# Raw weight blocks placed in another pool and requested at another point, and eight plain matmuls at a group's end

## The chip, the cores and the metric

One core of a Trainium2 chip runs the whole program. The metric is the device time of one execution in microseconds; the number used for a kernel is the median over its runs. A profile of one execution shows what every engine does: TensorE (PE, with its weight loads as PEld), VectorE (DVE), ScalarE (ACT), GpSimd (POOL), SyncE (SP) and the DMA queues that SP and POOL issue to.

## What is computed

Three layers follow each other. First a linear recurrence per head over 768 steps with complex decays (4 batches, 8 heads, head size 48), then a layer that sends each of 3072 tokens to one of 8 experts, then a product of two projections followed by two more weight matrices:

```python
# layer 1: S is 48x48 per batch and head
for t in range(768):
    new_re = ar * S_re - ai * S_im          # ar, ai: a_re, a_im, cut to magnitude 0.999
    new_im = ar * S_im + ai * S_re
    S_re, S_im = new_re + outer(k[t], v[t]), new_im
    y[t] = q[t] @ S_re
# layer 2: for the tokens of expert e (argmax of x @ w_gate), gate = softmax value of that expert
out[mask] = gate * (relu(x[mask] @ w1[e]) @ w2[e])       # 384 -> 1024 -> 384
# layer 3
h = ((x @ w1) * (x @ w2)) @ w3                           # 384 -> 1024, then 1024 x 1024
return h @ w_out                                         # 1024 -> 384
```

The weights of layer 3 come as float64.

## The kernel before

**Layer 1** is done by two streams that `drive` interleaves in the program's order. The stream `first` (`Attn.elementwise`, L803) goes through 24 pieces of 8 time steps: it forms the decay coefficients `cf` (L840) from `a`, `sq` and `y0`, multiplies them up to prefix products `P` (L861, L863), scales queries and keys by them into `qk` (L903) and stores that to DRAM as `qkd` (POOL L910 and L912, for the last half piece SP L916 and L917 and POOL L918). The tiles `a`, `sq`, `y0` and `cf`, which the text calls the multipliers' memory, live in the pool `e`; `P`, `pr`, `s2` and the raw queries and keys live in the pools `e2` and `qk`.

The stream `second` (`Attn.groups`, L1126) goes through three groups of the sequence, each of 8 units of 64 steps for 2 batches. A unit loads `vz` and `kk` (L1007, L1009, on SP), transposes `kk` (L993) into `qkT` (ACT L994), forms scores in the PSUM tile `sc` (L1021) which DVE masks (L1025), and forms the outputs `y` (L1040, L1041; the last matmul is remembered as `self.lasty`). Units are tied by a state `W` in PSUM: PE adds the last state by L1078, ACT copies it out (`z`, L1079), PE adds the unit's keys and values (L1085), ACT and DVE multiply it by the decays (L1092, L1093, L1094), and L1078 of the next unit waits for that. A group can start when its 8 pieces are stored (`made`); at its start `ends` (L967) transposes the last prefixes and, ahead of the second and of each earlier group only (`g < NG - 1`), runs 8 plain matmuls named `dense`, whose result nobody reads. Finished rows are routed to their experts by `route` (L111) and scattered by POOL (L162).

**Layer 3's inner product**, `w3 @ w_out`, is formed ahead of layer 2 by the class `Fuse`. Its inputs are 24 raw float64 blocks: 8 of `w_out` (384 KB each) and 16 halves of `w3` (512 KB each). SP loads a raw block (`doubles`, L291) into one of five buffers `fdr`; `halves` (L313) makes two float32r parts of it with six DVE operations (L336, L337, L339, then L322, L323, L324) and two of ACT (L329, L330); this is called a split below. `ahead` (L278) keeps up to four loads ahead of the split that is being written. The first 16 splits (8 of `w_out`, 4 pairs of `w3`) are taken one or two at a time by the third group's loop (L1165 to L1167), the other 8 behind the last routing. `_bound` (L711) places every DVE operation of the first 16 splits behind `S.end`, the last `qk` multiplication (L903).

The pool `wf1` (`wp`) is opened by `factors`, when the 24th piece's prefixes are written into the program and the pool `e` is closed; in memory it takes the place of `e`. The pool `wf2` (`w2p`) is opened when `first` is through and takes the place of `e2` and `qk`. In the kernel before, `wf1` holds both parts of all eight `w_out` factors and one pair of `w3` parts, `wf2` holds the five raw buffers and three pairs of `w3` parts.

**The order of work** on each engine is fixed when the program is built: a scheduler takes each instruction as its inputs, its memory and its engine come free by its own model of time, earlier program lines first. Each engine then runs its list in order, waiting where an input is not there. So an SP load that waits for a buffer holds up the loads behind it, and a DVE split that waits for a raw block holds up the chain's DVE operations behind it.

After the last unit, PE runs the product of six `w3` blocks (L729), then the experts with the rest of the product in between (L478), and then layer 3 (L538).

Of the kernel before, what the change touches and what calls it, by code (L numbers as in the profile page):

```python
# [9 lines left out]
F32 = mybir.dt.float32  # L10
F32R = mybir.dt.float32r
# [10 lines left out]
DM = 384  # L22
# [3 lines left out]
NF = 8  # L26
# [6 lines left out]
RAW = 4  # L33
# [241 lines left out]
        yield  # L275


def ahead(load, srcs, n):  # L278

    got = []  # L280
    for i in range(len(srcs)):
        while len(got) < min(i + n, len(srcs)):
            got.append(load(srcs[len(got)]))
        yield got[i]


def doubles(pool, dma, bufs=RAW):

    def load(src):
        raw = pool.tile([128, 512, 2], I32, tag="fdr", name="fdr", bufs=bufs)[:, : src.shape[-1]]  # L290
        dma.dma_start(raw.rearrange("p n c -> p (n c)"), src.bitcast(I32))  # L291
        return raw

    return load
# [18 lines left out]
def halves(S, nc, raws, rest, units):  # L313

    v, act = nc.vector, nc.scalar
    first, second = [], []
    for n in range(len(units) + 2):
        if second:
            place, raw, m = second.pop()
            H, L = place()  # L320
            hi, lo = raw[:, :, 1].bitcast(F32), raw[:, :, 0].bitcast(F32)
            v.tensor_tensor(out=H, in0=hi, in1=m.bitcast(F32), op=ALU.mult)  # L322
            v.tensor_scalar(out=m, in0=H.bitcast(I32), scalar1=-0x800000, scalar2=None, op0=ALU.bitwise_and)  # L323
            v.scalar_tensor_tensor(out=L, in0=lo, scalar=2.0 ** -20, in1=m.bitcast(F32), op0=ALU.mult, op1=ALU.mult)  # L324
        if first:
            second.append(first.pop())
            _, raw, m = second[0]
            hi = raw[:, :, 1].bitcast(F32)
            act.activation(out=m, in_=m, func=AF.Relu, scale=8.0, bias=S.rebias)  # L329
            act.activation(out=hi, in_=hi, func=AF.Sign)  # L330
        if n < len(units):
            raw = next(raws)
            k = raw.shape[1]
            m = rest.tile([128, 512], I32, tag="fdm", name="fdm", bufs=2)[:, :k]
            low = rest.tile([128, 512], U16, tag="fdl", name="fdl")[:, :k]
            v.tensor_scalar(out=m, in0=raw[:, :, 1], scalar1=0x7FFFFE00, scalar2=None, op0=ALU.bitwise_and)  # L336
            v.tensor_scalar(out=low, in0=raw.bitcast(U16)[:, :, 2], scalar1=0x1FF, scalar2=None, op0=ALU.bitwise_and)  # L337
            lo = raw[:, :, 0]
            v.scalar_tensor_tensor(out=lo.bitcast(F32), in0=lo.bitcast(U32), scalar=2.0 ** -32, in1=low, op0=ALU.mult, op1=ALU.add)  # L339
            first.append((units[n], raw, m))  # L340
        yield
# [7 lines left out]
def mm3(nc, out, lh, ll, rh, rl, first, last):  # L349
    nc.tensor.matmul(out, lh, rh, start=first, stop=False)  # L350
    nc.tensor.matmul(out, lh, rl, start=False, stop=False)  # L351
    return nc.tensor.matmul(out, ll, rh, start=False, stop=last)  # L352


class Expert:


    def __init__(self, tc, S, wp, xp, hp, ps, py):
        self.nc, self.S = tc.nc, S
        self.wp, self.xp, self.hp, self.ps, self.py = wp, xp, hp, ps, py  # L360
# [79 lines left out]


def moe(tc, S, fuse, product):

    nc = tc.nc
    extra = moe2_weights(tc, S)
    with ExitStack() as pools:
# [55 lines left out]
        for x in (product, extra):  # L502
            for _ in x:
                pass
# [116 lines left out]
NH = 8  # L621
# [3 lines left out]
NG = 3  # L625
# [4 lines left out]
R2 = 2 * D  # L630
# [10 lines left out]
WARM = 8  # L641
# [30 lines left out]
class Fuse:  # L672


    def __init__(self, tc, S, wp, psum):

        self.tc, self.S, self.nc, self.wp = tc, S, tc.nc, wp
        self.psum = psum
        self.w2p = None
        self.ready = self.blocks = 0  # L680
        self.units = self._singles()

    def _singles(self):
        nc, S, wp = self.nc, self.S, self.wp
        self.wo = [wp.tile([128, NF, DM], F32R, tag=f"wo{x}", name=f"wo{x}") for x in "hl"]
        self.w3 = []

        def factor(f):
            return lambda: [x[:, f] for x in self.wo]

        def block(f, h):
            def place():
                if not h:
                    pool = wp if f % W3B == 0 else self.w2p
                    self.w3.append([pool.tile([128, NF, 128], F32R, tag=f"w3{x}{f % W3B}", name=f"w3{x}{f}") for x in "hl"])
                return [x.rearrange("p g c -> p (g c)")[:, h * 512 : (h + 1) * 512] for x in self.w3[f]]
            return place

        srcs = [S.w_out[f * 128 : (f + 1) * 128, :] for f in range(NF)]
        srcs += [S.w3[f, :, h * 512 : (h + 1) * 512] for f in range(NF) for h in range(2)]  # L700
        raws = ahead(doubles(self.w2p, nc.sync, 5), srcs, 4)
        first = [factor(f) for f in range(NF)] + [block(f, h) for f in range(W3B) for h in range(2)]
        rest = [block(f, h) for f in range(W3B, NF) for h in range(2)]
        for n, _ in enumerate(self._bound(halves(S, nc, raws, wp, first), lambda: [S.end])):
            self.ready = max((n - 1 - NF) // 2, 0)
            yield
        for n, _ in enumerate(self._bound(halves(S, nc, raws, wp, rest), lambda: S.gate)):
            self.ready = W3B + max((n - 1) // 2, 0)
            yield

    def _bound(self, steps, behind):  # L711
        while True:
            with ExitStack() as order:
                for x in behind():
                    order.enter_context(self.tc.issue_after(x.ins))
                if next(steps, self) is self:
                    return
            yield

    def product(self):  # L720
        nc = self.nc
        for f in range(NF):
            while self.ready <= f:
                next(self.units)
                yield 0
            wh, wl = self.w3[f]
            po = self.psum(f, f"wpo_{f}")
            for g in range(NF):
                mm3(nc, po[:, :DM], wh[:, g], wl[:, g], self.wo[0][:, g], self.wo[1][:, g], g == 0, g == NF - 1)  # L729
                if g % 2 and g < NF - 1:  # L730
                    if self.ready < min(f + W3B, BEFORE):
                        next(self.units)
                    yield 960
            ws = (self.wp if f % 2 else self.w2p).tile([128, DM], F32, tag="ws", name=f"ws_{f}")
            nc.scalar.copy(ws, po[:, :DM])
            nc.sync.dma_start(self.S.wf[f * 128 : (f + 1) * 128, :], ws)
            self.blocks = f + 1
            yield 960
# [38 lines left out]
class Attn:  # L777
# [251 lines left out]
    def outputs(self, u, v, z):  # L1029
        nc, S, st, pp = self.nc, self.S, self.st, self.pp  # L1030
        g, q, c = u
        nm = "%d%d%d" % u
        qkT, at = self.qkT.pop(u), self.at.pop(u)
        y = pp.tile([128, NH, D], F32, tag="y", name=f"y{nm}")
        for h in range(NH):
            for i in range(2):
                ps = slice(i * C, (i + 1) * C)
                nz = g == 0 and c == 0
                if not nz:
                    nc.tensor.matmul(y[ps, h], qkT[:, 0, h, ps], z[:, h // 4, i, h % 4], start=True, stop=False)  # L1040
                self.lasty = nc.tensor.matmul(y[ps, h], at[:, h], v[:, i, h], start=nz, stop=True)  # L1041
            if h == NH - 1:
                xt = S.rpool.tile([128, DM], F32, tag="xo", name=f"xo{nm}", bufs=S.xbufs)
                nc.scalar.copy(xt, y.rearrange("p h d -> p (h d)"))
                self.held.pop(u)
                self.xs.append((tuple((2 * q + i) * SEQ + (g * 4 + c) * C for i in range(2)), xt))
                if len(self.xs) == (RB if g == NG - 1 else RB0):
                    bank = lambda name: self.adds.tile([128, 512], F32, tag="ad", name=name, bufs=2)
                    at = max([n for n, x in enumerate(self.pool) if x.kind == "route"], default=0)
                    ids, xts = zip(*self.xs)  # L1050
                    number(self.tc, S, self.slot, ids)
                    self.pool.insert(at + 1, Item("route", self.route(self.slot, xts, bank)))
                    self.slot += len(self.xs)
                    self.xs = []
            if h % 2:
                yield 650
# [259 lines left out]
W3B = 4  # L1316
# [113 lines left out]
```

## Time and profile before

| what | us |
|---|---|
| median of 3 runs (lowest, highest) | 1000.34 (997.92, 1002.75) |
| the profiled execution, its own time | 1002.27 |
| its span, first to last instruction | 1000.6 |
| PE busy in the span | 900.3 |
| DVE busy in the span | 608.9 |
| ACT busy in the span | 488.9 |
| mean granted TensorE clock | 0.943 |

The span is read in stages: layer 1 up to 404.6 us, the inner product and the routing's end up to 434 us, the experts up to some 700 us, layer 3 to the end. A stage in which PE is busy nearly all the time can only become shorter by less PE work or a higher clock; in layer 1, PE is not, and the engine or the transfer that ends PE's idle time must be looked up for each stretch. The granted clock is given as a share of the higher of two levels: 1.00 is 2.4 GHz, 0.50 is 1.2 GHz, and a number in between says how much of the stretch lay at either.

### The profile page before, as it was taken

What the parts mean: (1) busy time and instruction counts of PE and PEld (TensorE: products, weight loads), DVE (VectorE), ACT (ScalarE), POOL (GpSimd) and SP (SyncE); (2) the same over time, 40 slices, a digit from 0 to 9 for tenths busy, and PEclk for the clock granted to TensorE, in tenths of its full rate; (3) what the DMA queues carried; (4) which work ended last, traced back from release to release, by engine and by line L of the source; (5) the groups of instructions that cost most, each with busy time, mean ns of one, the idle gap of its engine ahead of it and who ended that gap; (6) DMA issues with size and microseconds to landing.
All of it is one profiled execution on the core that took longest, in us unless ns stands there. A gap on an engine that the chain in (4) does not pass through costs nothing. (4 is left out here: it accounts for less than half of the span.)

```text
span 1000.6 us, 17074 instructions
## 1 busy us (share of the span) xinstructions
PE 900.3 (90%) x6402; PEld 769.4 (77%) x6402; DVE 608.9 (61%) x1378; ACT 488.9 (49%) x1092; POOL 129.1 (13%) x198
## 2 busy tenths in 40 slices
PE   3446799967998979999989999998999999999997
PEld 2222478746886868989979999997888888888886
DVE  6999899997993885666589995442232323232222
ACT  6555689865774766445456654443131313121211
POOL 5111000211020100100242211110000000000001
PEclk8766999978997999999999999999999999999999
DMA  6566975348728763644687745630000000000000
GB/s 221 179 206 236 293 247 172 122 128 290 226 112 279 215 216 102 204 141 122 183 222 173 205 113 136 138 68 2 1 9 24 9 24 9 24 7 27 9 24 31
DMA packets 90246, 128.74 MB, mean 129 GB/s; under 512 B 7264, under 2 KB 72720, under 8 KB 90160
## 3 DMA queue, kind: packets, MB, share of 16 engines
q1 hardware_dynamic: 76316, 82.42, 28.9%
q0 software_dynamic: 10736, 40.56, 11.6%
q10 hardware_dynamic: 3108, 4.65, 1.7%
q8 instruction: 51, 0.84, 0.3%
q14 instruction: 35, 0.29, 0.1%
HBM read 92.38 MB, written 35.22 MB: 128 GB/s over the span
## 5 line engine op out<-in xcount | busy, mean ns | idle before, releaser
L606 DVE TENSOR_TENSOR ab<-asb,pb 128x512 f32<-128x512 f32 x48 | 33.0, 687 | 189.8 <-PE pb L352 184.7
L345 ACT CAST h<-w 128x384 fp32r<-128x384 f32 x128 | 65.4, 514 | 96.8 <-PE ph L351 50.6
L346 DVE TENSOR_TENSOR l<-w,h 128x384 fp32r<-128x384 f32 x128 | 70.6, 555 | 63.3 <-ACT h L345 60.5
L601 ACT COPY asb<-pa 128x512 f32<-128x512 f32 x48 | 28.2, 587 | 122.6 <-PE pa L352 117.0
L345 ACT CAST gh<-ab 128x512 fp32r<-128x512 f32 x48 | 29.7, 620 | 95.2 <-DVE ab L606 95.2
L817 PE MATMUL x<-s,ident 128*128 128x384 f32 x64 | 36.0, 701 | 43.7 <-ACT s L876 43.7
L351 PE MATMUL py<-hl,h 128*128 128x432 f32 x192 | 70.7, 368 | 4.1 <-DVE hl L407 4.1
L993 PE MATMUL tr<-ident,kk 128*96 128x128 f32 x384 | 62.3, 298 | 10.5 <-DMA kk<-qkd 10.5
L350 PE MATMUL py<-hh,h 128*128 128x432 f32 x192 | 69.6, 363 | 2.2 <-ACT hh L406 2.2
L352 PE MATMUL py<-hh,l 128*128 128x432 f32 x192 | 69.6, 362 | 0.0
L350 PE MATMUL ph<-xh,h 128*128 128x432 f32 x192 | 69.1, 361 | 0.0
L352 PE MATMUL ph<-xh,l 128*128 128x432 f32 x192 | 69.1, 360 | 0.0
L351 PE MATMUL ph<-xl,h 128*128 128x432 f32 x192 | 68.9, 359 | 0.0
L861 DVE TENSOR_TENSOR pr<-cf,P 128x192 f32<-128x192 f32 x189 | 66.6, 353 | 3.3
L994 ACT COPY qkT<-tr 96x512 f32<-96x512 f32 x96 | 54.9, 593 | 23.3 <-PE tr L993 22.7
L351 PE MATMUL po<-ol,gh 128*128 128x384 f32 x192 | 65.0, 338 | 0.0
L350 PE MATMUL po<-oh,gh 128*128 128x384 f32 x192 | 64.8, 338 | 0.0
L352 PE MATMUL po<-oh,gl 128*128 128x384 f32 x192 | 64.0, 338 | 0.0
L570 POOL DMA_INDIRECT out<-ob,mdp x24 | 23.8, 992 | 307.4 <-DVE ob L569 165.6
L350 PE MATMUL pa<-yh,ah 128*128 128x512 f32 x144 | 57.3, 398 | 3.0 <-ACT yh L345 3.0
L993 PEld LDWEIGHTS tr<-ident,kk 128*96 128x96 f32 x384 | 44.4, 138 | 19.8 <-DMA kk<-qkd 8.4
L817 PEld LDWEIGHTS x<-s,ident 128*128 128x128 f32 x64 | 14.9, 258 | 58.1 <-ACT s L876 50.8
(219 smaller groups left out, 2410.8 us busy)
## 6 DMA issues: line engine op xcount, KB each, us to landing
w<-in_w SPq DMA_DIRECT2D x128, 192.0 KB, 2.6
kk<-qkd SPq DMA_DIRECT2D x24, 768.0 KB, 7.6
qkd<-qk POOLq DMA_DIRECT2D x21, 768.0 KB, 5.7
qkr<-in_qk SPq DMA_DIRECT2D x24, 384.0 KB, 6.5
a<-in_a SPq DMA_DIRECT2D x11, 768.0 KB, 5.6
fdr<-in_w SPq DMA_DIRECT2D x16, 512.0 KB, 5.6
fdr<-in_v POOLq DMA_DIRECT2D x12, 512.0 KB, 6.9
xs<-zr POOLq DMA_DIRECT2D x8, 648.0 KB, 7.2
```

The lines of the kernel that those rows point to most:

```text
L345: nc.scalar.copy(H, src)
L346: nc.vector.tensor_tensor(out=L, in0=src, in1=H.bitcast(F32), op=ALU.subtract)
L350: nc.tensor.matmul(out, lh, rh, start=first, stop=False)
L351: nc.tensor.matmul(out, lh, rl, start=False, stop=False)
L352: return nc.tensor.matmul(out, ll, rh, start=False, stop=last)
L570: nc.gpsimd.indirect_dma_start(out=S.outv[j], out_offset=bass.IndirectOffsetOnAxis(ap=S.mdp[:, j, 0:1], axis=0), in_=ob, in_offset=None, b ...
L601: nc.scalar.copy(asb, pa)
L606: nc.vector.tensor_tensor(out=ab, in0=asb, in1=pb, op=ALU.mult)
L817: nc.tensor.matmul(p, S.ident, s[r], start=r == 0, stop=r == 1)
L861: v.tensor_tensor(out=pr, in0=twice(cf[i][:, t]), in1=bc(pv, 2, 1), op=ALU.mult)
L993: nc.tensor.transpose(pt[:, h], qk[:, h0 + h, w], self.S.ident)
L994: nc.scalar.copy(qkT[:, w, h0 : h0 + 4], pt)
```

## The change

The five raw buffers move from `wf2` to `wf1`, and the first five loads are written into the program as soon as `wf1` is open, ahead of the last piece's keys and stores and of the third group's loads. To make room, the factors 4 to 7 of `w_out` and the pair of `w3` parts that lay in `wf1` move to `wf2`. The splits themselves, their order in the program and their place behind `S.end` stay as they are. Besides, behind the last output of the second group's last unit (`u == (1, 1, 3)`), eight matmuls of 512 columns are added that write to a tile in the bank of the scores; nobody reads it.

```diff
-def ahead(load, srcs, n):
-
-    got = []
+def ahead(load, srcs, n, got=()):
+
+    got = list(got)
...
         self.w2p = None
         self.ready = self.blocks = 0
+        self.srcs = [S.w_out[f * 128 : (f + 1) * 128, :] for f in range(NF)]
+        self.srcs += [S.w3[f, :, h * 512 : (h + 1) * 512] for f in range(NF) for h in range(2)]
+        self.load = doubles(wp, self.nc.sync, RAW + 1)
+        self.first = [self.load(x) for x in self.srcs[: RAW + 1]]
         self.units = self._singles()
...
-        self.wo = [wp.tile([128, NF, DM], F32R, tag=f"wo{x}", name=f"wo{x}") for x in "hl"]
+        n = NF // 2
+        self.wo = [[p.tile([128, n, DM], F32R, tag=f"wo{x}", name=f"wo{x}{i}") for x in "hl"] for i, p in enumerate((wp, self.w2p))]
...
-                    pool = wp if f % W3B == 0 else self.w2p
-                    self.w3.append([pool.tile([128, NF, 128], F32R, tag=f"w3{x}{f % W3B}", name=f"w3{x}{f}") for x in "hl"])
+                    self.w3.append([self.w2p.tile([128, NF, 128], F32R, tag=f"w3{x}{f % W3B}", name=f"w3{x}{f}") for x in "hl"])
...
-        srcs = [S.w_out[f * 128 : (f + 1) * 128, :] for f in range(NF)]
-        srcs += [S.w3[f, :, h * 512 : (h + 1) * 512] for f in range(NF) for h in range(2)]
-        raws = ahead(doubles(self.w2p, nc.sync, 5), srcs, 4)
+        raws = ahead(self.load, self.srcs, RAW, self.first)
...
             if h == NH - 1:
+            if h == NH - 1 and u == (NG - 2, 1, 3):
+                w = pp.tile([128, 512], F32, tag="sc", name="dense2")
+                for _ in range(WARM):
+                    with self.tc.issue_after(self.lasty.ins):
+                        S.warm = nc.tensor.matmul(w, S.ident[:R2], qkT[:, 0, :4].rearrange("e h t -> e (h t)"), start=True, stop=True)
```

## Rows read from the trace of the kernel before

**Rows 1.** Windows by stage: start:end, busy us (instructions) by engine, clock, DMA share, GB/s.

```profile
core 0: us, PE busy (x) PEld busy (x) DVE busy (x) ACT busy (x) POOL busy (x), PEclk, DMA share, GB/s
299.00:306.30 7.30, 7.02 (x89) 5.75 (x87) 5.66 (x15) 4.16 (x15) 1.08 (x2) 0.77 0.50 190
306.30:310.70 4.40, 3.63 (x80) 3.42 (x80) 0.40 (x1) 2.28 (x9) 0.55 (x1) 1.00 0.59 140
310.70:314.20 3.50, 0.03 (x1) 0.06 (x2) 1.02 (x2) 1.61 (x4) 0.00 (x0) 0.77 1.08 338
314.20:326.20 12.00, 12.00 (x53) 10.21 (x53) 3.54 (x15) 4.74 (x9) 0.00 (x0) 0.50 0.97 328
326.20:344.00 17.80, 17.80 (x300) 15.34 (x300) 16.41 (x44) 14.90 (x40) 4.33 (x4) 1.00 0.72 223
...
356.00:388.00 32.00, 28.79 (x376) 23.24 (x378) 26.22 (x68) 22.77 (x53) 3.61 (x3) 0.89 0.47 155
388.00:404.60 16.60, 16.02 (x250) 13.28 (x250) 4.49 (x15) 7.51 (x19) 3.19 (x4) 1.00 0.30 102
404.60:434.00 29.40, 28.64 (x179) 27.91 (x176) 19.45 (x51) 13.30 (x26) 2.17 (x2) 1.00 0.69 218
434.00:500.00 66.00, 64.11 (x345) 60.60 (x343) 40.09 (x88) 31.67 (x66) 5.84 (x9) 1.00 0.49 143
```

**Rows 2.** PE's timeline: start us, us, line, operation, count [idle before <-releaser].

```profile
310.34 0.32 PE L1041 MATMUL y<-vz,at 128*64 128x48 f32 x4
314.17 1.06 PE L993 MATMUL tr<-ident,kk 128*96 128x128 f32 x4 [3.51 <-DMA kk<-qkd]
...
323.50 2.77 PE L1085 MATMUL W<-vz,kk 128*96 128x96 f32 x16
...
336.09 1.52 PE L1085 MATMUL W<-vz,kk 128*96 128x96 f32 x16
```

**Rows 3.** Waits from 310 to 405 us: engine line <- releaser, total us, times, longest.

```profile
DVE fdl L337 <- DMA fdr<-in_w: 6.2, 4, 2.2
...
PE W L1078 <- DVE W L1094: 6.0, 2, 3.2
```

**Rows 4.** PE's timeline at the starts of the first and the second group.

```profile
102.74 7.13 PE L983 MATMUL dense<-qk,ident 128*128 128x512 f32 x16 [1.93 <-DVE qk L903]
...
218.40 9.81 PE L983 MATMUL dense<-qk,ident 128*128 128x512 f32 x16 [2.35 <-DVE qk L903]
```

**Rows 5.** SP's timeline around the third group's start.

```profile
306.28 0.34 SPq L916 DMA_DIRECT2D qkd<-qk  x1
...
308.17 3.39 SPq L1009 DMA_DIRECT2D kk<-qkd  x3
311.73 4.25 SPq L291 DMA_DIRECT2D fdr<-in_w_out  x5
...
326.30 0.38 SPq L1009 DMA_DIRECT2D kk<-qkd  x1
330.50 0.35 SPq L291 DMA_DIRECT2D fdr<-in_w_out  x1
```

**Rows 6.** DVE's timeline from the last piece into the first splits.

```profile
298.54 0.35 DVE L861 TENSOR_TENSOR pr<-cf,P 128x192 f32<-128x192 f32 x1
...
305.30 0.96 DVE L903 TENSOR_TENSOR qk<-P,qkr 128x768 f32<-128x768 f32 x1
310.30 0.55 DVE L1093 TENSOR_TENSOR cc<-W,T 96x384 f32<-96x384 f32 x1 [4.04 <-ACT cc L1092]
...
322.61 0.19 DVE L138 TENSOR_REDUCE mx<-lg 128x4 f32<-128x32 f32 x1 [10.89 <-ACT lg L133]
...
323.39 0.35 DVE L336 TENSOR_SCALAR fdm<-fdr 128x384 int32<-128x384 int32 x1
...
329.87 0.55 DVE L324 SCALAR_TENSOR_TENSOR wol<-fdr,fdm 128x384 fp32r<-128x384 f32 x1
```

**Rows 7.** The tile fdr: durations in ns, min/median/max, first and last start, forms.

```profile
L322 DVE TENSOR_TENSOR w3h<-fdr,fdm x16: 676/680/693, 357.2 to 468.0; 128x512 fp32r<-128x512 f32 x16
```

More of the change, by code (lines that the diff above doesn't have):

```diff
@@ L684, in _singles @@
         nc, S, wp = self.nc, self.S, self.wp
-        self.wo = [wp.tile([128, NF, DM], F32R, tag=f"wo{x}", name=f"wo{x}") for x in "hl"]
+        n = NF // 2
+        self.wo = [[p.tile([128, n, DM], F32R, tag=f"wo{x}", name=f"wo{x}{i}") for x in "hl"] for i, p in enumerate((wp, self.w2p))]
         self.w3 = []
         def factor(f):
-            return lambda: [x[:, f] for x in self.wo]
+            return lambda: self.factor(f)
         def block(f, h):
@@ L709, in _singles, with factor @@
             yield
+    def factor(self, g):
+        return [x[:, g % (NF // 2)] for x in self.wo[g // (NF // 2)]]
     def _bound(self, steps, behind):
@@ L728, in product @@
             for g in range(NF):
-                mm3(nc, po[:, :DM], wh[:, g], wl[:, g], self.wo[0][:, g], self.wo[1][:, g], g == 0, g == NF - 1)
+                mm3(nc, po[:, :DM], wh[:, g], wl[:, g], *self.factor(g), g == 0, g == NF - 1)
                 if g % 2 and g < NF - 1:
```

## The prediction

> **What bounds the kernel now.** I read the stages first [rows 1]. From 404.6 us on PE is busy nearly without a break (28.64 of 29.4 us, then 64.11 of 66), so what follows layer 1 moves as a block: if layer 1 ends earlier, the product, the routing's end and the experts start earlier by the same amount. Nothing that the change touches lies behind that point except the place of some tiles. The question is therefore when the third group ends, at 404.6 us in this execution.
>
> The third group begins with a hole. The second group's last output starts at 310.34 us, and the next PE instruction, the transposes of the third group's first `kk`, starts at 314.17, released by the transfer of `kk` [rows 2]. In the 3.5 us of the hole PE does nothing, and in the 12 us behind it PE is busy all the time at a granted clock of 0.50 [rows 1], the lower level of 1.2 GHz. What that costs is read from one line at both levels: sixteen L1085 matmuls take 2.77 us there and 1.52 us later [rows 2], a ratio of 1.82.
>
> The rest of the group is bound by PE where it is not interrupted (17.80 of 17.80 us from 326.2 to 344, 16.02 of 16.6 us from 388 on), and by DVE where it is. The list of waits shows PE standing 6.0 us in two pieces at L1078 until DVE has multiplied `W`, and DVE itself standing 6.2 us in four pieces for raw blocks [rows 3]. From 356 to 388 us the clock is 0.89 on average [rows 1]: 0.11 x 2 x 32 = 7.0 us lie at the lower level, which costs 7.0 x (1 - 1/1.82) = 3.2 us.
>
> **The change part by part: the eight matmuls.** A float32 matmul here is two records; the same eight, issued in earlier groups' starts, are 16 records in 7.13 us at the full clock, and 9.81 us where the clock was low for part of them [rows 4]. The last of the four outputs of the 310.34 row ends at 310.7, the new tile waits for nothing (its bank's last reader is the masking that these outputs needed), and the clock is 1.00 up to there [rows 1]. I take 7.0 us: PE would be free for the transposes at 317.7 instead of 314.2. If the clock stays up, the 12.0 us behind become 12.0 / 1.82 = 6.6 us, and the point that PE reached at 326.2 is reached at 324.3: 1.9 us gained. Bounds: with 9.8 us for the matmuls it is 327.1, a loss of 0.9 us; if the clock fell all the same, the loss is the full 3.5 us, since 317.7 replaces 314.2. I take 1.9, because the clock is at 1.00 when the eight begin and no idle time lies on either side of them.
>
> **The raw loads.** SP issues five raw loads at 311.73, behind three `kk` loads at 308.17; the first split starts on DVE at 323.39 [rows 5, 6]. In the new place their memory is free, at the latest, when DVE has read the last `cf` (the last L861, 298.54 [rows 6]). Five loads of 384 KB are 1.97 MB. From 299 to 310.7 us the DMA engines moved 190 and then 140 GB/s, against 338 in the hole [rows 1]; the room is (338 - 190) x 7.3 + (338 - 140) x 4.4 = 1.95 MB, just what the five need. So they land by about 310, and nothing of the last `qk` stores and the first `kk` needs to move by more than a few tenths. SP is past its stores only at 306.28 [rows 5], so five issues of some 0.43 us (2.2 us) in front of them have a place.
>
> The splits stay behind `S.end`, which starts at 305.30 and takes 0.96 us. Behind it DVE is idle for 4.04 us, and for 10.89 us ahead of 322.61 [rows 6], 14.9 us in all. A split of 384 columns is six DVE operations of 0.35 to 0.55 us [rows 6], 2.7 us in all: the hole takes 14.9 / 2.7 = 5.5 of them, the five that have their data. ACT's share, two operations, lies beside it: ACT is busy 4.74 of 12 us there [rows 1].
>
> What this is worth is read from the later stretch. DVE does all 16 splits between 323 and 388 us now, and behind 388 (DVE 4.49 of 16.6 us) PE has no wait for DVE and the clock stays at 1.00 [rows 1, 3]. With five splits done ahead (5 x 2.7 = 13.5 us of DVE), the crowded stretch ends near 373 instead of 388. The two waits for `W` and the low clock behind them cost 6.0 + 3.2 = 9.2 us. Bounds: nothing is gained if the splits that are left stand as close to the chain as now, all 9.2 if the chain always finds DVE free. I take two thirds, 6.2 us: the later of the two waits falls into the stretch that is set free, the earlier one does not, and may stay in part. A split of 512 columns is longer (0.68 us for its L322 [rows 7]), so DVE remains well filled up to 373.
>
> Beside this: the tiles that change pools are written in the same instructions with the same sizes, and those that go to `wf2` (factors 4 to 7, one pair of `w3`) are needed only after the fifth split, when the last `qk` store has long left that memory. I cost that at nothing; without that cover it would be the wait for one store, as the raw loads now have it. The raw loads are moved past SP's last `qkd` stores and `kk` loads; what stands behind them in SP's list are those, and PE waits for them.
>
> **A rule that speaks against it.** The raw loads would share the time of 299 to 310 us with POOL's and SP's last stores. The Trainium skill, in DMA: Bandwidth & Descriptors, section Issuing engines are not separate DMA queues, says that transfers started by different engines run on the same 16 DMA engines and interleave. By that rule alone the stores and the first `kk` are stretched by what the five loads take. It is the second rival below.
>
> **The sum.** 1.9 + 6.2 = 8.1 us. The profiled execution took 1002.27 us (span 1000.6 and 1.7 around it), so this one would take 994.2; the median of the runs before is 1000.34, 1.9 below the profiled one, and the same saving from the median gives 992.2 us. The forecast's own range is 989.2 (both terms at their upper bounds, 1.9 + 9.2 = 11.1) to 995.3.
>
> **The rivals.** *Only the matmuls count.* The head start is eaten: raw block six and later still arrive at the pace of five buffers, SP and DVE wait for each other as now, and the two waits for `W` come back at other places. For it: DVE's four waits for raw blocks are already there [rows 3]. Against it: fewer splits are then left. The time is 1000.34 - 1.9 = 998.4 us, a little less if part of a wait goes.
>
> *The five loads collide.* SP's transfers stand in one line; if the five are issued so late that they are all in front of the last stores, these and the first `kk` come later by 1.97 MB at 338 GB/s = 5.8 us, so `kk` lands at 320.0 instead of 314.2. The eight matmuls cover it up to 317.7; 2.3 us of hole stay and eat the 1.9 us of the first term. With half of the second term left the time is 1000.34 + 0.4 - 3.1 = 997.6 us. The same holds if the splits don't start earlier because the builder's order leaves them behind the routing's operation at 322.61.
>
> *Slower.* The splits are drawn forward in DVE's list further than the data: the sixth raw block can be requested only when the first buffer is free, and if SP's list has that load behind the `kk` load that waits until 326.30 [rows 5], it lands some 5 us later, as the first ones did now, past 331. DVE, standing at that split from about 321 on, then holds back the scores' masking, which now comes at about 327, by 4 to 5 us. The hole brings a stretch at the lower clock, 1.5 us as behind each of the two present waits. Two such stops are 2 x (4.6 + 1.5) = 12.2 us; less the first term and half of the second, 12.2 - 1.9 - 3.1 = 7.2 us slower, 1007.5 us. It decides from the point where a refill is issued later than DVE's head start lasts.
>
> **How the numbers follow.** A difference of about 0.5% (5 us) is what a measurement of this kernel can tell from no change. Chances: the forecast 0.53, of which 0.04 lies below 987 (the 989.2 of its bounds less the 2.4 us by which single runs before stood from their median); only the matmuls 0.21, of which 0.03 ends past 5 us of gain; collision or splits left in place 0.15; slower 0.11. So faster by over 0.5% has 0.56, within it 0.33, slower 0.11. The likeliest time is 992.2 us. For 8 in 10 the range takes in the forecast but its lowest tail, both rivals of little change, and leaves out most of the slower one: 987 to 1002.
>
> **What would show it.** Right: after the second group's last output a row of 16 records of 7 us and no wait for `kk` behind it; the clock at 1.00 from there through the first transposes; the five loads on SP before the last `qkd` store; the first L336 near 306.5 us; the fifteenth or sixteenth split at about 373 us; less than 3 us of waits at L1078; the product's first matmul near 396 us. Wrong: a clock of 0.50 behind the eight; `kk` landing after 318; the first split still at 320 or later; DVE waiting over 8 us for raw blocks; or a product that starts earlier and then waits for the routing, the factors or the experts' weights, so that the gain is given back before 500 us.

## The result

| kernel | median, us | lowest to highest |
|---|---|---|
| before | 997.92 | 994.75 to 1002.75 |
| changed | 1008.32 | 1006.05 to 1010.68 |

The changed kernel is slower: the ratio is 1.0105, with a 95% interval of [1.0085, 1.0126]. The forecast was 992.2 us and a range of 987 to 1002. So neither the sign nor the range held, and the time lies where the third rival put it (1007.5 us).

The profiled execution of the changed kernel took 1006.06 us, among the lowest of its runs, while that of before took 1002.27, among its highest. The two traces therefore show only 3.8 of the 10.4 us. Single executions of one kernel lie up to 5 us from their median here: traces say where time lies, and only the medians say how much it is.

### The profile after

The stages, in the stretches of [rows 1] (columns as there), in the changed kernel:

```profile
core 0: us, PE busy (x) PEld busy (x) DVE busy (x) ACT busy (x) POOL busy (x), PEclk, DMA share, GB/s
306.30:310.70 4.40, 3.52 (x71) 2.99 (x70) 4.31 (x12) 3.94 (x13) 0.62 (x1) 1.00 1.04 392
310.70:314.20 3.50, 3.50 (x26) 1.86 (x23) 3.50 (x9) 1.74 (x6) 0.00 (x0) 1.00 0.28 65
314.20:326.20 12.00, 10.35 (x63) 7.21 (x61) 8.90 (x25) 6.91 (x18) 0.00 (x0) 1.00 1.08 339
326.20:344.00 17.80, 15.74 (x252) 13.49 (x251) 15.96 (x43) 12.73 (x34) 7.35 (x4) 0.90 0.83 272
...
356.00:388.00 32.00, 29.74 (x439) 24.58 (x435) 17.32 (x45) 20.07 (x49) 4.04 (x4) 0.95 0.53 166
388.00:404.60 16.60, 13.88 (x186) 10.95 (x186) 4.62 (x14) 6.16 (x18) 1.94 (x2) 1.00 0.06 23
```

The hole of 3.5 us is filled, and the clock is 1.00 through the 12 us behind it where [rows 1] had 0.50. DVE has only 17.32 us of work from 356 to 388, where it had 26.22. All three were wanted. But PE has become idle in stretches where it was full or nearly so: 1.65 us from 314.2 to 326.2, 2.06 from 326.2 to 344, 2.72 from 388 on.

PE at the group's start (columns of [rows 2]; the lines are numbered by the changed kernel, where L1078 is L1088, L1079 L1089, L1085 L1095, L993 L998, and L1094 L1104):

```profile
311.18 7.13 PE L1051 MATMUL dense<-qkT,ident 96*128 96x512 f32 x16
...
319.07 1.51 PE L1088 MATMUL W<-cc,perm 96*96 96x384 f32 x4
320.41 1.04 PE L998 MATMUL tr<-ident,kk 128*96 128x128 f32 x8
...
323.92 1.60 PE L1095 MATMUL W<-vz,kk 128*96 128x96 f32 x16 [1.65 <-ACT z L1089]
...
328.45 0.41 PE L149 MATMUL rk<-oh,upper 128*128 128x32 f32 x2 [2.06 <-DVE oh L145]
...
333.08 1.73 PE L1088 MATMUL W<-cb,perm 96*96 96x384 f32 x4
```

The eight matmuls take 7.13 us, as the row they were costed by [rows 4], and nothing waits for `kk` behind them. One unit of the chain lies between two L1088: 333.08 - 319.07 = 14.0 us. In the kernel before it is nearly the same, though the first half of it lay at the lower clock:

```profile
317.67 2.77 PE L1078 MATMUL W<-cc,perm 96*96 96x384 f32 x4
...
332.43 1.46 PE L1078 MATMUL W<-cb,perm 96*96 96x384 f32 x4
```

That is 14.8 us. So the clock alone didn't set the pace of this unit. One trace of each says little on the size of it: further traces have 17.0 and 14.2 us for the changed kernel (e4 and e12 below) and 14.5 and 15.0 us for the one before (e0 and e8). DVE's rows show what stands in the unit's way in the changed kernel:

```profile
306.76 0.35 DVE L336 TENSOR_SCALAR fdm<-fdr 128x384 int32<-128x384 int32 x1
...
317.79 0.35 DVE L336 TENSOR_SCALAR fdm<-fdr 128x384 int32<-128x384 int32 x1
320.53 0.36 DVE L337 TENSOR_SCALAR fdl<-fdr 128x384 uint16<-128x384 uint16 x1 [2.38 <-DMA fdr<-in_w_out]
...
327.07 0.36 DVE L336 TENSOR_SCALAR fdm<-fdr 128x384 int32<-128x384 int32 x1 [1.27 <-DMA fdr<-in_w_out]
...
329.40 0.55 DVE L1103 TENSOR_TENSOR cb<-W,T 96x384 f32<-96x384 f32 x1
...
330.51 0.95 DVE L1104 TENSOR_TENSOR W<-W,T 96x768 f32<-96x768 f32 x1
...
349.68 0.43 DVE L337 TENSOR_SCALAR fdl<-fdr 128x512 uint16<-128x512 uint16 x1 [2.88 <-DMA fdr<-in_w]
```

The first split comes at 306.76, in the idle time that was meant for it, and DVE then runs ahead until it has used up the five early blocks. There it stands for the sixth block, and again at 327.07, with the chain's two multiplications queued behind. ACT's list stands with it. Its `z` could be copied when L1088 ended (320.6), but is listed behind the split's ACT operations:

```profile
322.13 0.62 ACT L329 ACTIVATE fdm<-fdm,rebias 128x384 int32<-128x384 int32 x1 [2.55 <-DVE fdm L336]
322.66 0.53 ACT L330 ACTIVATE fdr<-fdr 128x384 f32<-128x384 f32 x1
323.09 0.78 ACT L1089 COPY z<-W 96x768 f32<-96x768 f32 x1
```

Why the sixth block is late is in SP's issues (columns as in [rows 5]; L921 and L922 are L916 and L917 of before, L1014 is L1009):

```profile
299.54 3.99 SPq L291 DMA_DIRECT2D fdr<-in_w_out  x5
...
306.87 0.34 SPq L921 DMA_DIRECT2D qkd<-qk  x1
307.27 0.81 SPq L922 DMA_DIRECT2D qkd<-qk  x1
312.35 1.01 SPq L1014 DMA_DIRECT2D kk<-qkd  x2
313.46 1.24 SPq L291 DMA_DIRECT2D fdr<-in_w_out  x1
```

The five early loads leave SP at 299.54. `kk` has to wait for the `qkd` stores and is issued at 312.35, 4.2 us later than the 308.17 of [rows 5] (0.6 us of that is the last `qk` multiplication, which came later), and the refill stands behind it. Its buffer was free from about 311.1 on, when the first split's L324 ended, so its place in the list cost the refill 2.4 us, about as long as DVE's first stop.

PE's waits from 310 to 405 us in the changed kernel, as the list of [rows 3]:

```profile
PE rk L149 <- DVE oh L145: 4.3, 2, 2.3
PE W L1088 <- DVE W L1104: 2.7, 1, 2.7
PE W L1095 <- ACT z L1089: 1.7, 1, 1.7
PE y L1046 <- DVE at L1030: 1.1, 1, 1.1
```

The 6.0 us of waiting for `W` fell to 2.7 and the 3.5 us for `kk` are gone, but waits of 4.3, 1.7 and 1.1 us took their place.

### A ledger of the third group

One row per kernel, over the third group alone (from the end of the second group's last `y` to the end of the third's), makes the kernels comparable. Before, then changed:

```profile
310.70:404.80 94.10, 83.82 (x1125) 70.67 (x1125) 60.56 (x162) 58.93 (x144) 11.14 (x10) 0.89 0.62 200
```

```profile
311.20:409.00 97.80, 87.17 (x1143) 70.60 (x1141) 58.86 (x151) 56.78 (x140) 13.33 (x10) 0.95 0.55 175
```

The group's length is PE's idle time (length less PE busy), plus 0.45 of the time at the lower clock (that time is twice the length times 1 less PEclk; 0.45 is 1 - 1/1.82, by the ratio of [rows 2]), plus the added matmuls, plus the rest, which is the same work for all. Before: 10.3 + 0.45 x 20.7 + 0 + 74.5. Changed: 10.6 + 0.45 x 9.8 + 7.1 + 75.7. The rest is between 73.6 and 77.2 us in all 20 profiles of this study, and the clock is rounded to 0.01, which can move the second term by 0.4 us. Where the eight matmuls are added, the mean of the rest changes by no more than 0.3 us (the table of the halves below). So they cost their whole 7.1 us, and pay only with idle time or low clock that they remove.

### The profile page after: what moved, and what is told of

Its sections match the earlier page's. It is cut to its first block, busy times and chain, and to the rows that moved or that the text cites. A ratio compares the mean times of both kernels' runs of the same rounds, so it can differ in the third digit from the quotient of the medians.

```text
span 1004.3 us, 17103 instructions
## 1 busy us (share of the span) xinstructions
PE 901.7 (90%) x6418; PEld 768.4 (77%) x6418; DVE 611.6 (61%) x1378; ACT 488.4 (49%) x1092; POOL 128.6 (13%) x198
## 5 line engine op out<-in xcount | busy, mean ns | idle before, releaser
L998 PE MATMUL tr<-ident,kk 128*96 128x128 f32 x384 | 59.8, 290 | 7.0 <-DMA kk<-qkd 7.0
L999 ACT COPY qkT<-tr 96x512 f32<-96x512 f32 x96 | 54.9, 593 | 22.6 <-PE tr L998 22.1
L822 PEld LDWEIGHTS x<-s,ident 128*128 128x128 f32 x64 | 14.8, 257 | 59.2 <-ACT s L881 51.9
L352 PE MATMUL pa<-yh,al 128*128 128x512 f32 x144 | 57.3, 398 | 0.0
```

The lines of the kernel that those rows point to most:

```text
L822: nc.tensor.matmul(p, S.ident, s[r], start=r == 0, stop=r == 1)
L998: nc.tensor.transpose(pt[:, h], qk[:, h0 + h, w], self.S.ident)
L999: nc.scalar.copy(qkT[:, w, h0 : h0 + 4], pt)
```

## The experiments

All ratios are to the kernel before on the same chip, in the same comparison. Theory A: the stops for refilled raw blocks, in the lists of DVE and ACT, cost what the early blocks and the eight matmuls earn. Theory B: the matmuls themselves are a pure delay. Theory C: the loss lies in the list order that the builder makes, whatever the edit.

### The two halves

The matmuls alone are the last hunk of the diff put into the kernel before; the raw blocks alone are the change without that hunk. Both were run in three comparisons, in the first two beside a copy of the kernel before, in the third beside the change.

> The kernel before once more, for a second trace of it. Both theories: within 0.5% of its median of 997.9 us. Its earlier profiled execution (1002.3) was its slowest of seven; the question is which waits of the third group are shorter here: if the 3.5 us hole at the group's start or the 12 us at the lower clock are not there in a faster execution, the eight matmuls had less to win than was forecast.

> The kernel before with the eight matmuls alone; raw blocks as before. Theory A (splits drawn forward crowd the chain of the third group, DVE stands for raw blocks in front of the chain's operations): this half of the change is harmless, 1.9 us faster by the forecast's first term, 996 us, within 0.5%. Theory B (the eight matmuls cost more than the hole and the clock give back, because the group's chain and not PE sets its pace): slower by 3 to 7 us, 1001 to 1005 us.

> The change without the eight matmuls: raw blocks in the multipliers' memory, loaded sooner. Theory A: most of the loss is here, 5 to 10 us slower than before (1003 to 1008 us), with PE waiting in the third group behind DVE operations that stand behind a raw block. Theory B: not slower, 992 to 998 us.

> The kernel before for a third trace, beside the two halves alone. All theories: its own median within 0.3%. To be read from it: the length of the third group (from the second group's last output to the third's), 94 and 92 us in the two traces so far.

> The eight matmuls alone, again, beside the raw blocks alone. Theory B (they cost their 7 us less the hole, nothing comes back): if the chip is the kind on which the change lost 0.9%, 0.3 to 0.6% slower than before. Theory D (the loss is the meeting of both halves: the sixth raw block comes too late for splits that were drawn forward, and ACT's and DVE's lists have the chain behind them): within 0.2% of before.

> The raw blocks alone, again. Theory B: not slower than before, 0 to 0.4% faster. Theory D: some of the loss, since the splits are drawn forward here too and the sixth raw block is as late: 0 to 0.5% slower. In the trace, the first unit (from its first L1088 to the next) should be as long as in the change, 13 to 17 us, though the clock is low at its start.

> The change itself again, on one chip with its two halves. If the loss belongs to the change, it is 5 to 11 us slower than before here too (ratio 1.005 to 1.011); if it belongs to the chip of the earlier comparison, where before took 997.5 us and not 1004, the ratio is within 0.3% of 1 on a chip where before takes 1004.

> The eight matmuls alone. Two earlier comparisons gave +1.4 and +3.8 us. If the two halves of the change add up, matmuls only and raws only together give the change's difference on this chip within 3 us. If the loss is made by the two together (the matmuls delay the first W, and the sixth split then stands in front of it), the change loses 4 us or more beyond their sum.

> The raw blocks in their new place without the matmuls. Two earlier comparisons gave -2.1 and -1.1 us. Same reading as for the matmuls alone: additive halves leave the change at the sum of the two, an interaction leaves it 4 us or more above.

| kernel | first | second | third |
|---|---|---|---|
| copy of before | 1.0013 [0.9986, 1.0039] | 1.0004 [0.9968, 1.0040] | |
| matmuls only | 1.0014 [0.9987, 1.0040] | 1.0039 [1.0011, 1.0066] | 1.0001 [0.9975, 1.0027] |
| raw blocks only | 0.9979 [0.9954, 1.0004] | 0.9989 [0.9953, 1.0024] | 0.9981 [0.9957, 1.0006] |
| the change | | | 1.0075 [1.0042, 1.0108] |

Neither half gains what was forecast, and neither loses much. Together they lose: the sum of the halves in the third comparison is 0.9982, and the change is 0.9% (about 9 us) above it. The loss isn't one of the chip or the comparison either: before took 1003.61 us here and 997.92 in the first result, and the change lost in both. A theory that adds the parts up is out. So is B as it was put for e1 (3 to 7 us of loss by the matmuls alone; they cost 0.1 to 3.9), and so is the first form of A (5 to 10 us of loss by the raw blocks alone; by the ratios they gained 1.1 to 2.1). What is left of A is a loss by the two together, which e9's expectation calls D.

The ledger, each figure a mean of three profiles (before, e0 and e8; e1, e9 and e13; e2, e10 and e14; the changed kernel, e4 and e12), in us:

| kernel | length | idle | low clock, x 0.45 | matmuls | rest |
|---|---|---|---|---|---|
| before | 93.8 | 10.0 | 9.3 | 0 | 74.5 |
| matmuls only | 90.4 | 5.8 | 3.3 | 7.1 | 74.2 |
| raw blocks only | 89.7 | 7.9 | 6.2 | 0 | 75.5 |
| the change | 100.0 | 10.0 | 7.6 | 7.1 | 75.3 |

Alone, the matmuls earn 10.3 us of idle time and clock in this group for their 7.1, and the raw blocks 5.2 for nothing. Together they earn 1.7 for 7.1. The rows of the third comparison, matmuls only, raw blocks only and the change:

```profile
311.30:401.80 90.50, 83.52 (x1138) 67.13 (x1137) 60.94 (x159) 58.51 (x144) 12.18 (x8) 0.98 0.64 204
```

```profile
315.80:407.40 91.60, 82.96 (x1126) 68.94 (x1125) 57.86 (x151) 56.69 (x140) 10.91 (x10) 0.90 0.58 186
```

```profile
315.50:418.20 102.70, 92.88 (x1141) 74.54 (x1141) 58.71 (x151) 56.78 (x141) 10.18 (x10) 0.89 0.52 166
```

The clock share tells it at a glance: 0.98 with the matmuls alone, 0.89 with the raw blocks beside them (0.96 twice against 0.95 and 0.91 in the other traces). What the matmuls bought is gone again.

One part of it belongs to the raw blocks alone and lies behind the splits. From the group's sixth L1088 on (L1083 in e13) no split is left in DVE's list in these two traces, the first of the change and e13, matmuls only:

```profile
378.90:409.00 30.10, 26.53 (x379) 21.92 (x377) 7.35 (x20) 12.11 (x33) 3.89 (x4) 0.94 0.07 28
378.90:401.80 22.90, 22.50 (x351) 18.50 (x349) 6.81 (x18) 11.48 (x31) 1.95 (x2) 1.00 0.09 36
```

PE stands idle for 3.6 us there, and so it does in all three traces of the change and all three of the raw blocks alone; it is 0.4 us with the matmuls alone and 0.6 in the kernel before, in three traces each. No stop for a raw block can be the reason of these 3 us; what in the lists is, was not found. They are gone in the versions e6 and e15 below (0.3 and 0.5 us), so a good part of what those win back lies here.

### No refills

The splits go round the first five blocks of 512 KB again and again; the later raw loads are left out.

```diff
-        self.first = [self.load(x) for x in self.srcs[: RAW + 1]]
+        self.first = [self.load(x) for x in self.srcs[NF : NF + RAW + 1]]
-        raws = ahead(self.load, self.srcs, RAW, self.first)
+        raws = (self.first[i % (RAW + 1)][:, : x.shape[-1]] for i, x in enumerate(self.srcs))
```

> The changed kernel, but raw blocks after the fifth are left out: the splits go round the same five blocks, so no split after the fifth waits for a transfer and SP has no refills among its kk and vz loads. (All five are the 512 KB size.) Theory A, if the stops are those for refills: the waits of DVE for raw blocks go, and the time falls by 5 us or more below the changed kernel's 1008, to 1003 or less. Theory B, or if the stops are the splits' own work in DVE's list: about 1008, within 3 us.

Measured: 1.0028 [1.0005, 1.0051]. The first unit of the chain took 10.8 us, but the second 21.6, where the change had 14.0 and 14.2 in its first trace. The change was not in this comparison; against its 1.0075 to 1.0105 elsewhere, most of the loss goes with the refills, but this run alone could not show it. Without any stop for a raw block in its first two units, the kernel still isn't faster than before.

### The change again, half the matmuls, and the chain first

The second is the change with `range(WARM // 2)`. The third and fourth put the third group's chain ahead of everything else in the builder's list, in the change and in the raw blocks alone; the fifth does that in the kernel before, in the comparison of e8 to e10.

```diff
-            for x in self.chain(u, ld.pop(u)):
+            steps = self.chain(u, ld.pop(u))
+            while True:
+                with self.tc.high_priority(HP) if g == NG - 1 else nullcontext():
+                    x = next(steps, None)
+                if x is None:
+                    break
```

> The changed kernel once more, on a chip on which the others of this set and the kernel before run too. If the loss belongs to the kernel and not to the chip of the first comparison: slower than before by 0.5 to 1.2%. If it belongs to how that chip's transfers fall: within 0.4%, as the two halves alone were.

> The changed kernel with four plain matmuls in place of eight. Theory B (their time goes straight into the group, because the chain of units and not PE's clock sets its pace): 3.5 us less than the changed kernel. Theory C (the order in which the builder lists PE's work of the third group decides; it is another one here): anything from 2 us more to 8 us less, to be read from where the last unit's L1095 stands in the list; here it stands behind sc, y and rk as in the changed kernel, so by C the group's second half stays as long as in the changed kernel.

> The changed kernel with the chain's operations of the third group's units (W, z, cb) given a high priority in the builder's list. Theory C: the chain's matmuls come ahead of outputs and scores, the group's second half shortens by 4 us or more, the kernel by as much. Theory B: the first half's length stays, since it is the eight matmuls; the whole gains less than 2 us.

> Raw blocks as in the change, no plain matmuls, chain first in the list. Theory C: faster than the raw blocks alone by 4 us, so some 6 us faster than the kernel before. Theory B: as the raw blocks alone, 2 us faster than before.

> The kernel before with the third group's chain put first in the builder's list, nothing of the change. Theory C (the list's order is the larger lever): 0.3% or more faster than before; if so, what the change with the chain first won over the change is not the change's own matter. Theories B and D: within 0.2% of before, because its lists have no splits that stand for a sixth block in front of the chain.

Measured: the change 1.0091 [1.0068, 1.0113], so the loss repeats; four matmuls 1.0074 [1.0055, 1.0094]; the change with the chain first 1.0014 [0.9996, 1.0032]; the raw blocks with it 0.9986 [0.9960, 1.0011]; before with it 1.0133 [1.0071, 1.0195].

Half the matmuls save 3.5 us of PE, and about half of that arrives: 2.0 us between the medians, 2.3 in the group's length, with intervals of the ratios that overlap. The group's clock share was 0.91 in e4 and in e5, and idle time 9.7 and 9.6. "Chain first" takes the loss away, but not by the stop: `z` still came 11.6 us behind the second group's end (11.9 in the changed kernel), and DVE still stood twice for a raw block in front of the first unit's multiplication of `W`, which ended 20.2 us behind that end (20.3):

```profile
318.97 0.36 DVE L337 TENSOR_SCALAR fdl<-fdr 128x384 uint16<-128x384 uint16 x1 [2.13 <-DMA fdr<-in_w_out]
...
325.60 0.36 DVE L336 TENSOR_SCALAR fdm<-fdr 128x384 int32<-128x384 int32 x1 [1.37 <-DMA fdr<-in_w_out]
...
329.15 0.95 DVE L1104 TENSOR_TENSOR W<-W,T 96x768 f32<-96x768 f32 x1
```

What went was idle time and low clock further on (7.6 us idle, clock 0.96). So these two stops can stand there without the loss. The same edit costs the kernel before 1.3% and does nothing for the raw blocks alone, where C had forecast a gain of 0.3% or more and one of 4 us. What stands of C is that order alone moves this kernel by about 1%; the direction it had right for the change only.

### Taking one stop away

Here the splits from the sixth on, with the last operations of the fourth and fifth, are put behind one instruction of the third group's first unit. All loads and all work stay. In e15 it is the unit's last multiplication (L1104); e16 is the same without the matmuls; in e17 it is only the first `z` (L1089).

```diff
-        for n, _ in enumerate(self._bound(halves(S, nc, raws, wp, first), lambda: [S.end])):
+        for n, _ in enumerate(self._bound(halves(S, nc, raws, wp, first), lambda: [S.end] + ([S.chain] if self.begun >= RAW + 1 else []))):
+            self.begun = n + 1
...
-        nc.vector.tensor_tensor(out=lanes(na), in0=lanes(W), in1=T(0).unsqueeze(3).to_broadcast([R2, 2, NH, D]), op=ALU.mult)
+        last = nc.vector.tensor_tensor(out=lanes(na), in0=lanes(W), in1=T(0).unsqueeze(3).to_broadcast([R2, 2, NH, D]), op=ALU.mult)
+        if u == (NG - 1, 0, 0):
+            S.chain = last
```

> The change with every split from the sixth on placed behind the third group's first unit (its last product of W by the decays). If the stop at the sixth raw block ahead of the first z is what costs, the first z follows its W at once, the second unit's first W comes 2.5 us earlier or more (at most 19.3 us behind the second group's end instead of 21.8), and the whole takes 3 to 6 us less than the change in the same comparison. If the splits' refills only move the same stops to later units, or the order of the tail sets the end, the second W is earlier but the whole takes within 2 us of the change.

> The splits from the sixth on behind the first unit, and no eight matmuls. If the matmuls' delay of the first W (7.8 us behind the second group's end against 3.2 without them) is never given back, this takes 3 to 5 us less than the same with the matmuls did, so 0.996 to 0.999 of before. If the matmuls' time is covered once the chain isn't stopped, it is 1.000 to 1.003 as with them.

> The change with the splits from the sixth on only behind the first z. If the stop in front of this one z is what costs, the time is 5 us or more below the change's, 1.000 to 1.004 of before. If it is DVE's place for the whole first unit (the product of W by the decays behind a split that waits for its raw block), it stays at 1.006 to 1.010.

Measured: e15 1.0018 [0.9985, 1.0050], in the comparison where the change had 1.0075; e16 1.0010 [0.9983, 1.0037]; e17 1.0116 [1.0095, 1.0136]. In e15, PE's two L1088 (here L1089):

```profile
323.43 1.51 PE L1089 MATMUL W<-cc,perm 96*96 96x384 f32 x4
...
332.59 1.46 PE L1089 MATMUL W<-cb,perm 96*96 96x384 f32 x4
```

The first unit takes 9.2 us, and 14.2 in the change's trace of the same comparison; the second takes 12.9 instead of 18.5. The group's row:

```profile
315.60:407.60 92.00, 84.85 (x1138) 69.13 (x1137) 57.96 (x148) 56.88 (x140) 11.09 (x8) 0.96 0.58 180
```

Against the change in the same comparison, idle time falls from 9.8 to 7.2 us, and the lower clock from 22.6 to 7.4 us, worth 6.8: by the ledger the matmuls now pay for themselves. e16 fits that: without them the hold gives 1.0010, no better than 1.0018 with them, so the 3 to 5 us that a lasting delay would have cost aren't seen; with these intervals, of two comparisons, 3 us are not ruled out. DVE still waits for later blocks, 8.8 us in all (6.5 in the change's trace) and 3.5 at the longest, but with more of the group behind it.

The first unit of e16, of e15 and, beside them, of e13 (matmuls only, nothing drawn forward), from one L1088 to the next (L1084, L1089 and L1083 in these kernels):

```profile
312.10:328.80 16.70, 15.01 (x87) 11.91 (x88) 9.20 (x30) 8.10 (x21) 4.25 (x4) 0.50 1.05 320
323.40:332.60 9.20, 8.69 (x97) 7.62 (x97) 4.73 (x20) 5.11 (x16) 0.00 (x0) 1.00 1.00 286
319.60:336.70 17.10, 13.89 (x167) 11.48 (x166) 15.52 (x48) 13.00 (x32) 0.00 (x0) 0.90 0.82 262
```

Where the later splits are held back, the unit does follow PE's clock, in one trace each: 16.7 us at 0.50 without the matmuls, 9.2 at 1.00 with them, a ratio of 1.82. In e13 it takes 17.1 us at a clock of 0.90, with DVE at work for 15.5 of them.

In e17 `z` follows 9.4 us behind the second group's end, as in e15, and nothing is won; the time even lies above the 1.006 to 1.010 that was expected for that case. DVE's rows:

```profile
320.27 0.36 DVE L337 TENSOR_SCALAR fdl<-fdr 128x384 uint16<-128x384 uint16 x1 [3.33 <-DMA fdr<-in_w_out]
...
327.35 0.36 DVE L337 TENSOR_SCALAR fdl<-fdr 128x384 uint16<-128x384 uint16 x1 [3.84 <-DMA fdr<-in_w_out]
...
330.49 0.55 DVE L1106 TENSOR_TENSOR cb<-W,T 96x384 f32<-96x384 f32 x1
...
331.78 0.95 DVE L1107 TENSOR_TENSOR W<-W,T 96x768 f32<-96x768 f32 x1
```

Two stops, 7.2 us together, stand ahead of the unit's multiplications, which end 23.4 us behind the second group's end; in e15 it was 15.8. So the late ACT copy, which looked like the cause in the trace, is not: taking the stop from in front of it alone changed nothing. It is tempting to put the loss on the other place, in front of the multiplication of `W`. But the matmuls alone have that multiplication as late, and lose nothing; in e13, where the second group ends at 311.3:

```profile
333.31 0.95 DVE L1099 TENSOR_TENSOR W<-W,T 96x768 f32<-96x768 f32 x1
```

It ends 23.0 us behind the second group's end there, 19.0 to 21.3 us in the three traces of before and 19.0 to 21.8 in the three of the change. So what is shown is that the loss hangs on where the splits from the sixth on stand in the lists: holding them behind the first unit gives back 0.6% of the 0.75%, with intervals that overlap by a little. That the stops in front of the first unit's multiplication are what costs is not shown, and e6, e13 and the idle time behind the last split speak against it.

No version tried beats the kernel before by more than its interval.

## Why the prediction was wrong

**Right.** The matmuls' 7.13 us, the clock of 1.00 behind them, no wait for `kk`, the first split near 306.5 (306.76), the last of 16 at about 373 (its L324 started at 371.68), under 3 us of waits at L1078 (2.7), and that what follows layer 1 moves as a block (from the product's first matmul to layer 3 it took 285.7 us before, 285.3 after). But that first matmul came at 408.9 us, not near 396, and one of the signs of being wrong is there: DVE waited 8.5 us for raw blocks from 310 to 405 us, where 8 were named (6.2 before).

**The first term, 12.0 us to 6.6.** The step that failed is "If the clock stays up, the 12.0 us behind become 12.0 / 1.82 = 6.6 us". The clock stayed up, and the unit still took 14.0 us in the first trace (17.0 and 14.2 in the other two) against 14.8 (14.5, 15.0) before, and 17.1 to 17.5 with the matmuls alone. PE's clock was one of two paces there. The other, as far as the traces show, was that of DVE's and ACT's lists with the splits in them, which the term put at nothing; only with the later splits held back does the forecast's ratio come out, 16.7 us to 9.2. Measured, the matmuls alone are worth 0.1 to 3.9 us of loss, not 1.9 of gain.

**The second term, two thirds of 9.2 us.** The raw blocks alone brought 0.1 to 0.2%, 1.1 to 2.1 us, and not 6.2. The waits at L1078 did fall as forecast. Two things were left out. When the five early blocks are used up, DVE comes to the sixth at 318.1 us in the changed kernel, 2.4 us ahead of its data. And from the group's sixth L1088 on, behind the last of these splits, PE stands idle for 3 us more than before, for a reason that is not known.

**The loads' place on SP.** "Nothing of the last `qk` stores and the first `kk` needs to move by more than a few tenths" failed. The room was worked out from bytes moved, 1.95 MB in 11.7 us, and the stores came in the part that was full: from 306.3 to 310.7 the DMA share was 1.04 at 392 GB/s, and `kk` was issued 4.2 us late. The Trainium skill, in DMA: Bandwidth & Descriptors, section Issuing engines are not separate DMA queues, says that transfers from different engines interleave on the same 16 DMA engines, and the trace agrees as far as it goes: the last store that POOL issues landed 5.5 us behind its issue beside the loads, and 3.1 us in the kernel before. The matmuls covered this for `kk`, as the second rival had it; for the refill behind `kk` nothing did.

**The sum.** This is the step that makes a loss out of two small terms. They were added as if each earned its own, and by the ledger they spoil each other's gain: 10.3 and 5.2 us of idle time and low clock alone, 1.7 together, against 7.1 us that the matmuls cost at once. In the whole time it is the 0.9% between 0.9982 and 1.0075. That the splits from the sixth on are what spoils it is shown by e15 for most of it; by which of their entries is open.

**The rival that came nearest** is "Slower", given 0.11. What it describes is in the trace: a refill issued behind `kk` while DVE stands at the split. Of its details, the stops are shorter (2.38 and 1.27 us, 2.88 and 1.43 later, 8.5 in all with the shortest, against 2 x 4.6), they stand ahead of the multiplication of `W` rather than the masking, and they aren't shown to be what costs. It was priced with half of the second term left, where the change has nothing left of it. That its 1007.5 us lies so near the 1008.32 is luck. The rows it needed were in [rows 5]: the refill loads stand in SP's list behind `kk`, and the five that come early are all that five buffers can bring.

Two slips in the sums, two thirds of 9.2 (6.1, not 6.2) and 388 less 13.5 (374.5, not 373), weigh nothing here.

**What stays open.** What the splits from the sixth on do to the matmuls' gain is not traced to single entries of the lists. In most runs the whole stands up to 6.5 us above what the group's length says (matmuls only: group 3.4 us shorter, whole 0 to 4 longer); only in e12 and e17 does it stand about 1 us below. Part of that is the choice of executions: five of the six profiled ones of the halves lay 0.8 to 5.1 us below their medians, the three of before 0.8 to 4.4 above; what else there is outside the group was not found. Why "chain first" helps one kernel and costs another 1.3% was followed only to idle time and clock, not to single entries of the list.

## What to carry to other kernels

When work is drawn forward into idle time, ask what it runs into when its head start ends: an in-order list stops at the first missing input, and everything behind stops too. Here, holding the pieces that had no data yet behind the chain took most of a loss away, though it gained nothing over the kernel before. An engine that is busy at a low clock isn't thereby the only bound: measure the distance between two steps of the chain at both clocks, in more than one trace, and with the other engines' lists out of the way. Gains that come from the same stretch must not be added before the two edits have run together. Matmuls that only keep the clock up are a debt of their full length until the whole time shows them paid; a ledger of one group showed 3.2 us of gain here, and the whole kernel none. And the operation that a wait is put down to needn't be the cause: try moving it before believing it.

## What the runs showed that was not expected

The kernel before took 997.92, 1004.56, 997.52, 1004.11, 1003.61 and 998.04 us (medians) in six comparisons: two levels, some 6 us apart, for one and the same program. The chip doesn't decide it, since 997.52 and 1003.61 are of the same one. Two profiles of before from the upper level have the second group's end at 316.7 and 318.7 us, the one from the lower at 310.7. Over all versions it is 308.1 to 311.2 us in the eight profiles of the lower level, and 315.5 to 318.7 in eleven of the twelve of the upper (311.3 in e13), so most of the 6 us lies ahead of the group that is studied here. Its cause was not sought; only ratios within one comparison are used for that reason.
